# Retention followed by a feed-forward layer: q and k of the later chunks turned by 32x32 squares on VectorE instead of by TensorE

## Chip, cores and metric

The kernel runs on one core of one Trainium2 chip. The metric is the time of one execution on the device in microseconds (us), the median of several runs; lower is better.

## What is computed

First comes a retention layer: attention without a softmax, in which the score of a query at place t and a key at place s is multiplied by gamma^(t-s), with a gamma of its own for each head, and is zero for s > t. Its output, laid out as one row of 512 numbers per token, goes through a feed-forward layer with a squared ReLU. All is float32.

```python
# q, k, v: (batch 8, heads 8, tokens 576, 64)
scores = q @ k.T / sqrt(64)
gamma  = 1 - 2 ** (-5 - head)
D[t, s] = gamma ** (t - s) if t >= s else 0
attn   = (scores * D) @ v
x      = attn.transpose(0, 2, 1, 3).reshape(4608, 512)
h      = maximum(x @ w_in, 0)          # w_in: (512, 2048)
out    = (h * h) @ w_out               # w_out: (2048, 512)
```

## The kernel before

**Tiling.** A batch entry of 576 tokens is cut into five chunks: four of 128 tokens and a short one of 64. That makes 40 chunks, numbered 0 to 39; 4, 9, 14 and so on are short. The decay is split into a factor gamma^t on q (with the 1/sqrt(64)) and a factor gamma^-s on v, so that scores need only a mask. For every pair of heads a 64x64 state in PSUM (`u_ps`, copied to `u_sb`) carries the sum over the keys of earlier chunks.

**The retention of one chunk** goes through these pieces, each a function of the kernel. `load` (L131) fetches q, k and v with the tokens on the partitions, three chunks ahead. `turn` (L379) brings q and k to the layout that the score products need, with two heads of 64 dimensions on the 128 partitions and the tokens along the row: 16 TensorE transposes of 64x64 blocks (8 for a short chunk, L387) write a PSUM tile `t_ps`; ScalarE copies the half with k out to `kT` (L393), and VectorE takes the half with q to `qT` (L397) while it multiplies it by a table `dq` of gamma^t, 128 x 4 x 576 numbers, that was loaded from DRAM by `load` of chunks 4 to 8 (L138). Only for chunks 0 to 3 q is multiplied before the transpose, tokens on the partitions, by `scale_q` (L374, the operation at L377), on GpSimd, with a small table `dv`; then `turn` only copies (L395). `scores` (L400) makes the products (L415); VectorE masks them into a tile `ret` (L420, L422), and GpSimd multiplies v by its decay (L424). `retain_a`, `retain_b` and `retain_c` multiply the masked scores with v (L436), add to the state (L439) and multiply the state with q (L471); ScalarE copies the state (L445) and the finished chunk of x (L493).

**The first feed-forward product** works on blocks of 512 tokens with a scheme of seven products in place of eight (`PRODUCTS`). Block 0 is done in the plain way (`first_in`) while the weights are being converted. For every other block there are 28 steps (`ffn_in`, L580): four passes of seven steps, each of eight 128x128 by 128x256 matmuls (L595) into one of three PSUM tiles `h_a`, `h_b`, `h_c`. Each step has its way out of PSUM: ScalarE at steps 0 and 3 (L605, L611, after which GpSimd squares, L612), VectorE at the others (L607, L609, L614, L618, L621, with the squares at L602). Between them VectorE works off further parts in small portions: sums of the hidden blocks (L533 to L536), sums of x (L519 to L522), and, in blocks 3 to 7, the conversion and sums of w_out (L210 to L248).

**Order.** The schedule is written by hand: each engine takes its instructions in the order of the program and waits for each one's inputs. One loop runs over the chunks. For chunks after 4 the pass i of it is

```python
retain_a(i - 1)
if i < N_CH:
    turn(i)
ffn(i - 1, 0)
retain_b(i - 1)
if i < N_CH:
    scores(i)
retain_c(i - 1)
ffn(i - 1, 1)
```

where each `ffn` runs some three or four steps of the feed-forward product, spread over the tokens by `PACE`. After the loop the rest of the steps run, and then the second product (`inner`, L866; about 390 us), which the change does not touch.

Of the kernel before, what the change touches and what calls it, by code (L numbers as in the profile page):

```python
# [15 lines left out]
C = 128  # L16
# [24 lines left out]
def kernel(  # L41
# [6 lines left out]
    moe_w_out: bass.AP,  # L48
    decay_q: bass.AP,
    decay_v: bass.AP,  # L50
    out: bass.AP,
# [79 lines left out]
    def load(i):  # L131
        b, ci, c0, cs = chunks[i]
        got = {name: pool.tile([128, H, D], F32, tag=name, name=f"{name}_ld") for name, pool in (("q", ld3), ("k", ld4), ("v", ld4))}
        if i == 0:
            nc.sync.dma_start(dv, decay_v)
        if N_EARLY <= i < N_EARLY + NCH:

            nc.sync.dma_start(dq[:, :, c0:c0 + cs], decay_q[:, :, c0:c0 + cs])  # L138
        for name, src in (("q", q), ("k", k), ("v", v)):
            t = got[name]  # L140

            issue = nc.scalar if i == 0 and name != "q" else nc.sync
            at = src[b, :, c0:c0 + cs, :].rearrange("h s d -> s h d")
            if name == "v":
                issue.dma_start(t[:cs], at)
            else:

                issue.dma_start(t[:cs, 0:H // 2, :], at[:, 0:H // 2, :])
                for e in range(2):
                    issue.dma_start(t[:cs, H // 2 + e::2, :], at[:, H // 2 + 1 - e::2, :])  # L150
        loaded[i] = [got["q"], got["k"], got["v"]]
# [168 lines left out]

    dq = only.tile([128, HP, S], F32, name="dq")
    dv = only.tile([128, H, 2 * NCH], F32, name="dv")
# [50 lines left out]

    def scale_q(i, engine):  # L374

        ci, t = chunks[i][1], loaded[i][0]
        engine.tensor_tensor(t, t, dv[:, :, NCH + ci:NCH + ci + 1].to_broadcast([C, H, D]), op=ALU.mult)  # L377

    def turn(i):  # L379

        cs, c0 = chunks[i][3], chunks[i][2]
        n_h = cs // CH
        p = ps_t.tile([128, 2, 512], F32, tag="t", name="t_ps").rearrange("p h (j d t) -> p h j d t", j=2, d=HP)
        for j in (1, 0):
            for hp in range(HP):
                for h in range(n_h):
                    nc.tensor.transpose(p[:, h, j, hp, :], loaded[i][j][rows(h), 2 * hp:2 * hp + 2, :],  # L387
                                        ident[rows(h), rows(h)])
        for j, name in ((1, "kT"), (0, "qT")):
            t = st[i][name] = work2.tile([128, HP, C], F32, tag=name, name=name) if j == 0 else work.tile([128, HP, C], F32, tag=name, name=name)  # L390
            to = t[:, :, :cs].rearrange("p d (h t) -> p h d t", h=n_h)
            if j:
                nc.scalar.copy(to, p[:, :n_h, j, :, :])  # L393
            elif i < N_EARLY:
                nc.vector.tensor_copy(to, p[:, :n_h, j, :, :])  # L395
            else:
                nc.vector.tensor_tensor(to, p[:, :n_h, j, :, :], dq[:, :, c0:c0 + cs].rearrange("p d (h t) -> p h d t", h=n_h),  # L397
                                        op=ALU.mult)

    def scores(i):  # L400
# [10 lines left out]
        for hp in range(HP):  # L411
            for h in range(n_h):
                for e in range(2):
                    t = slice(CH * h, CH * h + CH)
                    nc.tensor.matmul(sc[e][rows(h), hp, :], lhsT=kT[rows(e), hp, t], rhs=qT[rows(e), hp, t],  # L415
                                     start=True, stop=True, skip_group_check=True)
        r = st[i]["ret"] = work2.tile([128, 2, HP, CH], F32, tag="ret", name="ret")
        if i < N_EARLY:
# [258 lines left out]
    def ffn(i, half):  # L677

        gone[0] += chunks[max(0, min(i, N_CH - 1))][3] / 2
        if steps and steps[0][0] == 0:  # L680

            for f in (step, lambda: convert(6)) if half else (lambda: convert(6), step):
                f()
            if half and steps and steps[0][0] == 0:
                step()
                convert(6)
            return
# [9 lines left out]
        while steps and count:  # L697
            held[0] = half == 0 and count == 1
            step()
            count -= 1  # L700
# [16 lines left out]
    for i in range(N_CH + 1):  # L717
        if i <= N_EARLY:
# [29 lines left out]
            elif i == N_EARLY:  # L748
                convert(5)
                step()  # L750
                convert(6)
            if i < N_EARLY:
                if i + 1 < N_EARLY:
                    scale_q(i + 1, nc.gpsimd)
                if i < 2:
                    warm(6, False)
                turn(i + 1)
        else:
            if i == N_EARLY + 1:
                gone[0] = TOK  # L760
            retain_a(i - 1)
            if i < N_CH:
                turn(i)
            ffn(i - 1, 0)
            retain_b(i - 1)
            if i < N_CH:
                scores(i)
            retain_c(i - 1)
            ffn(i - 1, 1)
        if i == 0:  # L770
# [194 lines left out]
def _decays(B, H, S, D):  # L965


    import numpy as np

    gamma = 1.0 - 2.0 ** (-5.0 - np.arange(H))  # L970
    t = np.arange(S)
    n = -(-S // C)
    gt = gamma[:, None] ** t / math.sqrt(D)
    pairs = gt.reshape(H // 2, 2, 1, S).copy()
    pairs[H // 4:] = pairs[H // 4:, ::-1]
    gq = np.repeat(pairs, D, axis=2).reshape(H // 2, 2 * D, S).transpose(1, 0, 2)
    s = np.arange(n * C).reshape(n, C)
# [3 lines left out]
    gv = np.concatenate([gv, by_s], axis=2)  # L981
    return np.ascontiguousarray(gq, dtype=np.float32), np.ascontiguousarray(gv, dtype=np.float32)

# [31 lines left out]
```

## Time and profile before

| | |
|---|---|
| time, median of 3 runs | 994.51 us (994.42 to 995.4) |
| span of the profiled execution | 991.7 us |
| VectorE busy | 748.6 us, 75% |
| ScalarE busy | 190.4 us, 19% |
| GpSimd busy | 81.6 us, 8% |
| loop over the chunks | from the start to about 530 us |
| second product | from about 600 us to the end |

A busy share is an average over stages that are bound by different things. What a change in the loop over the chunks is worth has to be read from views of that stretch: which engine has no gaps there, how full the others are, and which wait ends last. The chain of waits is read backwards from the last instruction; an engine that is not on it has time to spare at that place.

### The profile page before, as it was taken

The page shows a single profiled execution, that of the slowest core. Times are in us where ns is not written, and L with a number is a line of the kernel's source. Part 1 is how long each engine was busy: PE and PEld are TensorE (multiplying, and loading weights), DVE is VectorE, ACT ScalarE, POOL GpSimd, SP SyncE. Part 2 cuts the span into 40 slices and gives each one's busy share as a digit, 9 for nine tenths or more (in the row PEclk, how much of TensorE's full clock was granted, in tenths as well). Part 3 has the DMA queues.
Part 4 walks back from the last instruction along what each step waited for, and adds up shares of the span by engine and source line. Part 5 has one row for each costly group of instructions (what it writes and reads, how often), then busy time and mean ns, then how long its engine had stood idle before and what let it go on. Part 6 is the DMA issues. An engine that isn't in the chain of part 4 may idle for free.

```text
span 991.7 us, 24441 instructions
## 1 busy us (share of the span) xinstructions
PE 973.5 (98%) x10532; PEld 869.5 (88%) x10532; DVE 748.6 (75%) x1427; ACT 190.4 (19%) x462; POOL 81.6 (8%) x85
## 2 busy tenths in 40 slices
PE   7899999999999999999999999999999999999998
PEld 7655688888888888888888889999999999999998
DVE  4688696567878888897886777777777777777765
ACT  3444222222222222223221010000000000000000
POOL 3100011111111111111111000000000000000000
PEclk9999999999999999999999999999999999999999
DMA  9984657665696878769458999675673757556351
GB/s 205 250 239 143 174 172 208 162 175 176 187 311 199 223 234 260 224 209 283 142 212 297 404 389 348 235 283 163 230 268 148 265 197 270 192 213 216 126 212 44
DMA packets 187676, 220.40 MB, mean 222 GB/s; under 512 B 119216, under 2 KB 137648, under 8 KB 178608
## 3 DMA queue, kind: packets, MB, share of 16 engines
q1 hardware_dynamic: 185456, 218.31, 67.8%
q8 instruction: 83, 1.36, 0.6%
q10 hardware_dynamic: 2112, 0.52, 0.2%
q14 instruction: 25, 0.20, 0.1%
HBM read 129.41 MB, written 89.39 MB: 221 GB/s over the span
## 4 chain that ended last, share of the span: by engine, by line
PE 91%; DVE 5%; DMA 1%; SPq 1%; issue 1%; ACT 1%; DVEq 0%; ACTq 0%
PE o_b L866 17%; PE h_b L595 16%; PE o_c L866 11%; PE o_a L866 11%; PE h_a L595 10%; PE h_c L595 10%; PE h_ps L559 5%; PE x_ps L436 3%; PE t_ps L387 2%; PE sc_ps L415 2%; PE x_ps L471 2%; DVE room L602 1%; PE u_ps L439 1%; DMA w<-in_moe_w_in_dram 1%; DMA w<-in_moe_w_out_dram 0%
## 5 line engine op out<-in xcount | busy, mean ns | idle before, releaser
L595 PE MATMUL h_b<-room,w 128*128 128x256 f32 x736 | 177.2, 383 | 1.2 <-DVE room L520 0.9
L595 PEld LDWEIGHTS h_b<-room,w 128*128 128x128 f32 x736 | 137.2, 190 | 21.4 <-PE t_ps L387 1.1
L866 PE MATMUL o_b<-w,room 128*128 128x128 f32 x1168 | 144.5, 275 | 0.2 <-DVE room L817 0.2
L866 PEld LDWEIGHTS o_b<-w,room 128*128 128x128 f32 x1168 | 137.2, 192 | 0.5 <-DVE room L817 0.4
L866 PE MATMUL o_c<-w,room 128*128 128x128 f32 x1008 | 123.0, 275 | 0.0
L866 PEld LDWEIGHTS o_c<-w,room 128*128 128x128 f32 x1008 | 117.7, 192 | 0.0
L595 PE MATMUL h_c<-room,w 128*128 128x256 f32 x480 | 114.4, 381 | 0.0
L595 PE MATMUL h_a<-room,w 128*128 128x256 f32 x448 | 107.6, 383 | 0.0
L595 PEld LDWEIGHTS h_c<-room,w 128*128 128x128 f32 x480 | 90.4, 190 | 12.6
L595 PEld LDWEIGHTS h_a<-room,w 128*128 128x128 f32 x448 | 83.7, 190 | 11.8
L866 PE MATMUL o_a<-w,a 128*128 128x128 f32 x688 | 85.6, 275 | 0.0
L866 PEld LDWEIGHTS o_a<-w,a 128*128 128x128 f32 x688 | 81.2, 192 | 0.1
L612 POOL TENSOR_TENSOR room<-room 128x512 f32<-128x512 f32 x32 | 35.2, 1100 | 438.2 <-ACT room L611 370.6
L602 DVE SCALAR_TENSOR_TENSOR room<-room 128x512 f32<-128x512 f32 x96 | 68.1, 710 | 3.3
L880 ACT COPY r<-o_a 128x128 f32<-128x128 f32 x53 | 14.1, 266 | 271.7 <-PE o_a L866 241.2
L559 PE MATMUL h_ps<-room,w 128*128 128x512 f32 (+1 forms) x160 | 60.1, 526 | 2.5 <-DVE w L228 1.7
L614 DVE TENSOR_TENSOR room<-h_b,room 128x512 f32<-128x512 f32 x32 | 22.1, 690 | 46.9 <-PE h_b L595 46.9
L436 PEld LDWEIGHTS x_ps<-ret,v_ld 64*64 64x64 f32 x1152 | 40.4, 136 | 15.9 <-issue 11.7
L436 PE MATMUL x_ps<-ret,v_ld 64*64 64x64 f32 x1152 | 50.0, 226 | 3.5 <-ACT u_sb L474 3.4
L559 PEld LDWEIGHTS h_ps<-room,w 128*128 128x128 f32 x160 | 30.3, 196 | 24.6 <-issue 19.1
L424 POOL TENSOR_TENSOR v_ld<-v_ld,dv 128x512 f32<-128x512 f32 (+1 forms) x40 | 42.8, 1075 | 63.5 <-DMA v_ld<-in_v_dram 58.6
L876 DVE TENSOR_TENSOR small<-o_b,small 128x128 f32<-128x128 f32 x62 | 18.1, 292 | 38.4 <-PE o_b L866 38.4
(109 smaller groups left out, 1377.4 us busy)
## 6 DMA issues: line engine op xcount, KB each, us to landing
g_dram<-room SPq DMA_DIRECT2D x32, 1792.0 KB, 7.7
a<-g_dram SPq DMA_DIRECT2D x43, 1024.0 KB, 7.1
room<-g_dram SPq DMA_DIRECT2D x20, 1024.0 KB, 6.4
w<-w_dram SPq DMA_DIRECT2D x7, 1792.0 KB, 13.0
out_dram<-room SPq DMA_DIRECT2D x17, 512.0 KB, 3.4
w<-in_moe_w_in_dram SPq DMA_DIRECT2D x16, 512.0 KB, 6.1
w<-in_moe_w_out_dram SPq DMA_DIRECT2D x16, 512.0 KB, 4.1
v_ld<-in_v_dram SPq DMA_DIRECT2D x31, 256.0 KB, 4.4
```

The lines of the kernel that those rows point to most:

```text
L387: nc.tensor.transpose(p[:, h, j, hp, :], loaded[i][j][rows(h), 2 * hp:2 * hp + 2, :], ident[rows(h), rows(h)])
L415: nc.tensor.matmul(sc[e][rows(h), hp, :], lhsT=kT[rows(e), hp, t], rhs=qT[rows(e), hp, t], start=True, stop=True, skip_group_check=True)
L424: nc.gpsimd.tensor_tensor(vs[:cs], vs[:cs], dv[:cs, :, ci:ci + 1].to_broadcast([cs, H, D]), op=ALU.mult)
L436: own.append(lambda hp=hp, e=e, b=b: nc.tensor.matmul(x_at(hp, b, h), lhsT=s["vs"][rows(h), 2 * hp + b, :], rhs=s["ret"][rows(h), e, hp, : ...
L471: nc.tensor.matmul(x_at(hp, b, h), lhsT=u[rows(e), hp, :], rhs=s["qT"][rows(e), hp, CH * h:CH * h + CH], start=clears(b, hp // 2), stop=Fa ...
L559: nc.tensor.matmul(p.rearrange("p h t -> p (h t)"), lhsT=w[:, c, :], rhs=xT[0][:, c, lo * HT:hi * HT], start=(c == 0), stop=(c == N_DM - 1))
L595: nc.tensor.matmul(p[:, mm, :], lhsT=w[:, c, :], rhs=xs[n][right][:, c, :], start=(j in OPENS and mm == 0 and c == 0), stop=(j in CLOSES a ...
L602: nc.vector.scalar_tensor_tensor(t, t, 0.0, t, op0=ALU.max, op1=ALU.mult)
L612: nc.gpsimd.tensor_tensor(g["A11"], g["A11"], g["A11"], op=ALU.mult)
L614: nc.vector.tensor_tensor(g["A22"], p, p15, op=ALU.add)
L866: nc.tensor.matmul(p, lhsT=s["lefts"][left][:, m, :], rhs=w_out[j][:, m, WO_SLOT[right], :], start=(i in OPENS and m == 0), stop=(i in CLO ...
L876: nc.vector.tensor_tensor(s["u2"], p, s["p1"], op=ALU.add)
```

## The change

From chunk 9 on, TensorE no longer turns q and k. VectorE transposes each 32x32 square of a chunk of k and of q in place (`flip`: two instructions per chunk, on all 128 partitions, into a tile `flip`), and ScalarE then carries each group of 32 partitions to the 32 partitions where it belongs (`spread`, `move`: 16 copies of 32 partitions x 256 numbers for a full chunk, 8 for a short one). The copies go into a list, from which three are issued ahead of every step of the feed-forward product (six while block 0 is still being worked on); the remainder is issued after the first half of the steps. `flip` and `spread` of a chunk run one pass of the loop ahead of the pass that uses them.

The multiplication of q by its decay is done for all chunks by `scale_q`, tokens on the partitions, on GpSimd, one pass ahead (chunk 0 stays on VectorE). The table `dq`, its memory and its five loads are gone; chunks 4 to 8, which TensorE still turns, are copied out of PSUM by VectorE without a product. q and k share one double-buffered tile `qk`, and the masked scores are written over the k half of it instead of into a tile of their own.

The purpose is to take the transposes off TensorE, and the table and its loads out of the kernel.

```diff
@@ load
-        if N_EARLY <= i < N_EARLY + NCH:
-            nc.sync.dma_start(dq[:, :, c0:c0 + cs], decay_q[:, :, c0:c0 + cs])
@@ scale_q and what follows it
+        ci, cs = chunks[i][1], chunks[i][3]
+        t = loaded[i][0][:cs]
+        engine.tensor_tensor(t, t, dv[:cs, :, NCH + ci:NCH + ci + 1].to_broadcast([cs, H, D]), op=ALU.mult)
+    N_TURN = 9
+    moves = []
+    def new_qk(i):
+        t = work2.tile([128, 2, HP, C], F32, tag="qk", name="qk")
+        st[i]["qT"], st[i]["kT"] = t[:, 0, :, :], t[:, 1, :, :]
+        return t
+    def flip(i):
+        cs = chunks[i][3]
+        t = st[i]["flip"] = work2.tile([128, 4, 2, HP, 32], F32, tag="flip", name="flip")
+        for j in (1, 0):
+            nc.vector.transpose(t[:cs, :, j, :, :], loaded[i][j][:cs].rearrange("s (p e) (d a) -> s (e d) p a", e=2, d=2))
+    def spread(i):
+        to = new_qk(i)
+        for b in range(chunks[i][3] // 32):
+            for g in range(4):
+                moves.append(lambda b=b, g=g: nc.scalar.copy(
+                    to[32 * g:32 * g + 32, :, :, 32 * b:32 * b + 32], st[i]["flip"][32 * b:32 * b + 32, g, :, :, :]))
+    def move(count):
+        for f in moves[:count]:
+            f()
+        del moves[:count]
@@ turn
-            if j:
-                nc.scalar.copy(to, p[:, :n_h, j, :, :])
-            elif i < N_EARLY:
-                nc.vector.tensor_copy(to, p[:, :n_h, j, :, :])
-            else:
-                nc.vector.tensor_tensor(to, p[:, :n_h, j, :, :], dq[:, :, c0:c0 + cs].rearrange("p d (h t) -> p h d t", h=n_h),
-                                        op=ALU.mult)
+        to = new_qk(i)[:, :, :, :cs].rearrange("p j d (h t) -> p j d h t", h=n_h)
+        nc.scalar.copy(to[:, 1].rearrange("p d h t -> p h d t"), p[:, :n_h, 1, :, :])
+        nc.vector.tensor_copy(to[:, 0].rearrange("p d h t -> p h d t"), p[:, :n_h, 0, :, :])
@@ scores
-        r = st[i]["ret"] = work2.tile([128, 2, HP, CH], F32, tag="ret", name="ret")
+        r = st[i]["ret"] = st[i]["kT"].rearrange("p (e a) (b t) -> p e (a b) t", e=2, b=2)
@@ ffn
+            move(6)
             for f in (step, lambda: convert(6)) if half else (lambda: convert(6), step):
                 f()
...
             held[0] = half == 0 and count == 1
+            move(3)
             step()
@@ the loop over the chunks
+            scale_q(i + 1, nc.gpsimd)
             if i < N_EARLY:
-                if i + 1 < N_EARLY:
-                    scale_q(i + 1, nc.gpsimd)
...
+            if i + 1 < N_CH:
+                scale_q(i + 1, nc.gpsimd)
             retain_a(i - 1)
-            if i < N_CH:
+            if i < N_TURN:
                 turn(i)
             ffn(i - 1, 0)
+            move(len(moves))
+            if N_TURN <= i + 1 < N_CH:
+                flip(i + 1)
             retain_b(i - 1)
             if i < N_CH:
                 scores(i)
             retain_c(i - 1)
+            if N_TURN <= i + 1 < N_CH:
+                spread(i + 1)
             ffn(i - 1, 1)
```

## Prediction before the run

> **What bounds the kernel now.** First the page: the busy times and the chain that ended last.
>
> ```profile
> PE 973.5 (98%) x10532; PEld 869.5 (88%) x10532; DVE 748.6 (75%) x1427; ACT 190.4 (19%) x462; POOL 81.6 (8%) x85
> PE 91%; DVE 5%; DMA 1%; SPq 1%; issue 1%; ACT 1%; DVEq 0%; ACTq 0%
> ```
>
> TensorE has no gaps to speak of. Taking work from it shortens the kernel, unless something else fills the gap. Next the windows of the stretch in which chunks 9 to 39 run. Columns: length, then busy us (and instructions) of PE, PEld, DVE, ACT, POOL, then clock, DMA share, GB/s.
>
> ```profile
> 105.00:237.50 132.50, 130.72 (x1699) 110.81 (x1699) 95.03 (x149) 30.83 (x71) 17.87 (x17) 1.00 0.63 178
> 237.50:512.50 275.00, 272.64 (x3407) 231.72 (x3406) 231.40 (x395) 71.89 (x155) 40.99 (x38) 1.00 0.73 220
> ...
> 387.50:400.00 12.50, 12.50 (x163) 10.36 (x163) 11.83 (x22) 2.42 (x6) 0.06 (x1) 1.00 0.61 163
> ...
> 425.00:437.50 12.50, 12.28 (x121) 10.02 (x122) 12.40 (x19) 2.04 (x4) 2.58 (x2) 1.00 0.50 164
> ```
>
> Two stretches: up to 237 us VectorE is 72% busy (95.0 of 132.5), from there to 512 us 84% (231.4 of 275; the conversion of w_out runs then), and single windows of 12.5 us are full. So TensorE sets the time, VectorE is a close second, ScalarE (26%) and GpSimd (15%) are far off. In the chain in order of time (start, length, what) a turn stands like this:
>
> ```profile
> 332.68 0.01 PE u_ps L439 x2
> 332.69 0.65 PE t_ps L387 x16
> 333.33 1.93 PE h_c L595 x8
> ```
>
> The turn costs the path 0.65 us, and the products after it take 1.93 us, as they do (1.92) where no turn precedes them. A short chunk's eight transposes show 0.64 too.
>
> **What the Trainium skill says.** (1) VectorE: DVE Perf Modes, "The three transpose paths": VectorE transposes 32x32 blocks only, a bf16 128x128 tile in 311 ns. Vector Engine (DVE) Microarchitecture Reference, 3.8: one element per cycle and lane. No transpose on VectorE is in this trace; its two-input products of 512 numbers take 682 to 692 ns, which fits one per cycle at the 0.96 GHz given there. (2) ScalarE: Activation LUTs, "What ACT_TABLE_LOAD costs": 186 ns + 0.833 ns per number, and 93 ns of overlap back to back; for 256 numbers 399 ns. The trace has 375 ns (from PSUM). (3) VectorE: DVE Perf Modes, "Two Vector instructions with no wait between them": the second SBUF read interface of VectorE is shared with GpSimd. The trace agrees; in order of time (start, length, engine):
>
> ```profile
> 430.80 1.11 POOL L612 TENSOR_TENSOR room<-room 128x512 f32<-128x512 f32 x1 [13.44 <-ACT room L611]
> 430.93 1.53 DVE L246 TENSOR_TENSOR w<-w 128x512 f32<-128x512 f32 x1
> 431.87 1.50 POOL L424 TENSOR_TENSOR v_ld<-v_ld,dv 128x512 f32<-128x512 f32 x1
> 432.38 1.54 DVE L247 TENSOR_TENSOR w<-w 128x512 f32<-128x512 f32 x1
> ```
>
> Two sums of 0.69 us took 1.53 beside GpSimd: each lost 0.84.
>
> **The change part by part.**
>
> TensorE: 31 turns (chunks 9 to 39) by 0.645 us leave: 20.0 us, 7.7 of it outside the full stretch (12 turns) and 12.3 within it (19 turns). Nothing is added.
>
> VectorE, per chunk: two transposes come, the product at L397 goes. Its row: 0.686 us (128x512, x28) and 0.420 (128x256, short chunks); back to back such instructions start 0.60 and 0.36 apart. A transpose of 512 numbers costs between 0.60 (one per cycle, overlapped) and 1.2 (4-byte numbers at half rate; nothing here rules it out). I take 0.65, because the skill's rate names no type. Full chunk: 1.3 - 0.6 = +0.7; short: 1.3 - 0.36 = +0.94. In the full stretch 16 x 0.7 + 3 x 0.94 = 14.0 us.
>
> GpSimd: 36 more products at 1.06 to 1.10 us (rows L424, L377) for chunks 4 to 39; it has the time. But each may run beside VectorE: from 0 to 0.84 us of VectorE's time, as above. GpSimd's work comes in a bunch just after L611, where VectorE often waits for step 4 (L614 waits 21.3 us in this stretch), so the first product is mostly hidden and a third one falls on busy time; I take 0.4. 19 x 0.4 = 7.6 us.
>
> VectorE's sum there: 231.4 + 14.0 + 7.6 = 253.0 us, against 275 - 12.3 = 262.7. It fits on average (96%), but not everywhere. A window of 12.5 us holds 0.86 chunks: it becomes 11.94 long and gets 21.6 / 22 = 0.98 us more. 425 to 437: 13.4 in 11.9; 387 to 400: 12.8; 262 to 275 (11.47 now): 12.45. Overrun 1.4 + 0.9 + 0.5 = 2.8 us. Nine more windows (10.8 to 10.9 now) end just full; 0.3 us each for uneven order inside: 2.7. So TensorE waits about 5.5 us more for VectorE there. Before 237 us only the window 120 to 130 is full (9.82 of 10): 0.8.
>
> ScalarE: 24 x 16 + 7 x 8 = 440 copies of 256 numbers, 0.31 (399 less 93) to 0.40 us each, 136 to 176 us, less 31 copies of k (0.585 and 0.373; 17 us), over some 400 us that hold 103 us now: 55 to 65%. Three copies ahead of a step (0.9 to 1.2 us) lie beside that step's 1.73 us of matmuls: hidden.
>
> Waits added. The first transpose waits for k's load, the second for `scale_q`, both a pass ahead; behind them on VectorE stand the mask of the scores and L614 or L607, for which TensorE waits before it may write that tile again. A transpose falls while TensorE does `retain_b`, `scores` and `retain_c` (0.62 + 0.47 + 0.5 us), where VectorE had only the mask: it lies well. `scores` waits for the last copy; behind it on TensorE is all that follows, but the copies end before the last steps of the half, so I cost it at nothing. `scale_q` waits for q's load; behind it are the product with v and the square at L612, needed a pass and some steps later. The copies wait for `retain_c` two chunks back, which ScalarE's copy of x (L493) waits for already. The mask written over k waits for products that it waits for anyway: nothing.
>
> The table: five loads (1.18 MB) go. One lies on the chain:
>
> ```profile
> 26.68 1.56 SPq L138
> ...
> 32.23 5.65 DMA w<-in_moe_w_in_dram
> 37.90 0.44 DVE w L210
> ...
> 40.73 0.59 ACT room L493
> 41.37 5.17 PE h_ps L559 x16
> ```
>
> The weights' load at 32.23 is issued behind L138; without it that is 1.67 us earlier (26.68 to 28.35, where the next issue starts), and TensorE, idle for about that load, starts earlier: 1.7 us.
>
> Sum: -20.0 + 5.5 + 0.8 - 1.7 = -15.4; 994.5 - 15.4 = 979.1, say 979 us.
>
> **Rivals.** (a) VectorE's extra work fits its gaps: its waits in the full stretch are 40 us (21.3 at L614, 6.2 at L397 for ScalarE's copy, which vanishes with L397). For it: gaps lie beside every step 4. Against: the full windows. Then -20.0 - 1.7: 973 us. (b) VectorE becomes the bound, because transposes of 4-byte numbers take 1.2 us and GpSimd costs the full 0.84. Full stretch: 231.4 + 16 x 1.8 + 3 x 2.04 + 19 x 0.84 = 282.3, and some 10 us of waits that can't be filled: 292, +17 on 275; outside -7.7 + 1.0 - 1.7: in all 1003 us, slower. For it: 84% now. Against: the skill's rate. With one of the two costs alone it ends near 990 to 995. (c) ScalarE comes late: its copies from SBUF in 0.5 us or more, so `scores` waits some 0.7 us in each of 31 passes, and steps wait for L605: 979 + 22 = 1001 us. Against: ScalarE's 26% now, and that `move` goes in threes.
>
> **Chances.** The main case 0.60 (975 to 987), (a) 0.12, (b) 0.22 (half of it slower than before), (c) 0.06. Low end 971: (a), and no dip of the granted clock after that early idle (a window from 40 to 45 us shows 0.66). High end 997: (b) with one cost. Beyond it lie the worst of (b) and (c), about 0.12. Faster 0.80, same 0.04, slower 0.16.
>
> **What would show it.** TensorE busy some 20 us less and no t_ps after chunk 8; transposes of 0.65 to 0.72 us in VectorE's groups; VectorE's busy time up by 20 to 30 us, windows from 237 us near 96%; waits of h_a, h_b, h_c for VectorE of some 5 us more; scores waiting for ScalarE under 2 us. Transposes of 1.2 us, many VectorE rows far above 0.69, or scores waiting for ScalarE in each pass would make it wrong.

## Result and profile after

The changed kernel takes 1007.34 us (median of 4 runs, 1007.13 to 1009.39), beside 994.95 us for the kernel before: ratio 1.0129, 95% interval 1.0111 to 1.0146. It is slower by 12.4 us where the forecast was faster by 15.4; the time lies outside the range of 971 to 997.

First the page's busy times. In the changed kernel L390 are the transposes on VectorE, L396 the copies between partitions, L433 the score products, L614 the matmuls of the feed-forward steps, L624 and L630 ScalarE's ways out of steps 0 and 3, and L493 ScalarE's small copy in `retain_b`.

```profile
PE 966.5 (96%) x10092; PEld 861.4 (85%) x10092; DVE 786.1 (78%) x1458; ACT 351.3 (35%) x871; POOL 128.7 (13%) x121
```

440 matmuls are gone. The span is 1007.7 us, so TensorE's gaps are 1007.7 - 966.5 = 41.2 us; before they were 991.7 - 973.5 = 18.2. That is +23.0. And TensorE's busy time fell by 7.0 us only, although turns of 20 us left: what remained became some 13 us longer. The two together are the 16 us between the spans; they are more than the 12.4 us between the medians, because the profiled execution is the slowest of the four (1009.39 us). The page's chain of waits answers nothing this time: its first piece lies at 604 us, after the loop over the chunks.

The windows of the kernel after, columns as in the prediction (length, busy PE, PEld, DVE, ACT, POOL, clock, DMA share, GB/s):

```profile
105.00:237.50 132.50, 125.91 (x1546) 106.14 (x1544) 100.66 (x154) 83.75 (x205) 30.59 (x27) 0.99 0.62 180
237.50:512.50 275.00, 257.94 (x2976) 217.25 (x2975) 245.19 (x394) 167.99 (x400) 63.76 (x55) 0.96 0.73 218
330.00:342.50 12.50, 12.45 (x111) 10.53 (x112) 8.07 (x14) 7.80 (x20) 0.00 (x0) 0.77 0.46 116
387.50:400.00 12.50, 12.27 (x152) 10.31 (x151) 10.70 (x18) 10.02 (x24) 4.08 (x4) 1.00 0.91 263
425.00:437.50 12.50, 9.41 (x132) 7.84 (x131) 12.36 (x20) 4.26 (x12) 2.68 (x2) 1.00 0.44 123
505.00:517.50 12.50, 9.80 (x116) 8.18 (x116) 6.33 (x11) 7.65 (x20) 3.06 (x3) 0.73 0.39 147
```

Three things stand here. TensorE is no longer full: 257.9 of 275 us, where it had 272.6. VectorE, which I had expected to be the new limit at 96%, is 89% busy (245.2 of 275), so in most places it is not what TensorE waits for. And the granted clock is 0.73 and 0.77 in single windows that had 1.00 before: after some gaps the matmuls run slower for a while. Over 5-us windows from 105 to 570 us, the time without a matmul sums to 24.0 us (before 4.5) and the lost clock, length times (1 - clock), to 11.9 us (before 0.0).

Who ended the gaps, from the list of waits between 105 and 570 us (engine and what it waited for: us in total, times, longest):

```profile
ACT qk L396 <- DVE flip L390: 27.8, 15, 5.7
...
PEld sc_ps L433 <- ACT qk L396: 19.0, 20, 3.7
PE sc_ps L433 <- ACT qk L396: 16.1, 19, 3.6
...
PE h_a L614 <- ACT room L624: 3.1, 1, 3.1
...
PE h_b L614 <- DVE room L539: 1.6, 1, 1.6
```

The score products wait for ScalarE's copies, 16.1 us in 19 waits. TensorE's waits for VectorE's ways out, the ones that I had priced, are small.

What the forecast took off TensorE did go. This is the timeline of the place where a turn stood in the chain before; the step follows the state's product directly.

```profile
366.51 0.23 PE L458 MATMUL u_ps<-v_ld,k_ld 64*64 64x64 f32 x2
366.66 1.99 PE L614 MATMUL h_b<-room,w 128*128 128x256 f32 x8
```

The start of ScalarE's small copy (L474 before, L493 after) marks each chunk in both traces. Where nothing waits, the interval from one chunk's mark to the next is 0.64 to 0.65 us shorter than before; others gain less, or lose up to 3.4 us (the one that ends with chunk 32 loses 3.40, with chunk 25 2.85, with chunk 36 2.60). From chunk 8 to chunk 39 the kernel falls 13.6 us behind (1.2 to 14.8).

The same stretch shows how an interval loses, here the one of chunk 27 (timeline, ScalarE and the score products, in order of time: start, length):

```profile
361.19 1.23 ACT L396 COPY qk<-flip 32x256 f32<-32x256 f32 x3 [1.46 <-DVE flip L390]
366.14 0.59 ACT L624 COPY room<-h_a 128x512 f32<-128x512 f32 x1 [3.72 <-PE h_a L614]
366.81 0.37 ACT L464 COPY u_sb<-u_ps 128x256 f32<-128x256 f32 x1
367.20 3.74 ACT L396 COPY qk<-flip 32x256 f32<-32x256 f32 x9
372.20 0.60 ACT L630 ACTIVATE room<-h_a 128x512 f32<-128x512 f32 x1 [1.25 <-issue]
...
372.56 0.30 PE L433 MATMUL sc_ps<-qk 64*64 64x64 f32 x4
372.82 1.65 ACT L396 COPY qk<-flip 32x256 f32<-32x256 f32 x4
...
373.69 0.32 PE L433 MATMUL sc_ps<-qk 64*64 64x64 f32 x2 [0.83 <-ACT qk L396]
...
374.52 0.62 PE L433 MATMUL sc_ps<-qk 64*64 64x64 f32 x25 [0.51 <-ACT qk L396]
```

ScalarE has idle time (3.72 us before L624), but it takes its work in the program's order: the copies stand behind ways out that wait for steps. Only four steps with three copies ahead of each lie here between the place where the sixteen copies enter the list and the end of the half, so four copies are left. They stand behind L630, the way out of the last step of that half, and the scores come right after that step. So the remainder runs while TensorE waits. At 507 us the same costs 3.56 and 0.36 us.

How often this happens can be counted from the order of the program: for eleven of the 31 chunks one to four copies are left when the half ends, 24 in all. The 19 waits of the scores fall on eleven chunks too, and ten of these are the same. The intervals in which these ten lie (they end with the small copies of chunks 10, 14, 15, 24, 25, 27, 29, 30, 34 and 36) fall 13.7 us behind together; in the other 21 from chunk 9 on, gains and losses cancel.

The largest single loss, chunk 32, is another one: the first copies are at the head of ScalarE's work before their transposes are done, and h_a's way out stands behind them.

```profile
434.73 1.23 ACT L396 COPY qk<-flip 32x256 f32<-32x256 f32 x3 [5.67 <-DVE flip L390]
435.99 0.59 ACT L624 COPY room<-h_a 128x512 f32<-128x512 f32 x1
...
436.63 2.43 PE L614 MATMUL h_a<-room,w 128*128 128x256 f32 x8 [3.09 <-ACT room L624]
```

Copies and transposes, from the groups by shape (busy, mean ns of one):

```profile
L396 ACT COPY qk<-flip 32x256 f32<-32x256 f32 x440 | 177.1, 402 | 34.2 <-DVE flip L390 27.8
```

```profile
L621 DVE SCALAR_TENSOR_TENSOR room<-room 128x512 f32<-128x512 f32 x96 | 75.5, 786 | 3.3
L222 DVE TENSOR_TENSOR w<-w,w 128x512 f32<-128x512 f32 x32 | 27.1, 846 | 0.6
...
L390 DVE STREAM_TRANSPOSE flip<-k_ld 128x512 f32<-128x512 f32 x24 | 16.8, 702 | 0.0
L390 DVE STREAM_TRANSPOSE flip<-q_ld 128x512 f32<-128x512 f32 x24 | 16.0, 667 | 0.0
```

Before, the first two rows were 710 and 688 ns (L602, L225). The timeline shows what lengthens them, as before:

```profile
424.71 1.50 POOL L373 TENSOR_TENSOR q_ld<-q_ld,dv 128x512 f32<-128x512 f32 x1
425.22 1.54 DVE L539 TENSOR_TENSOR room<-room 128x512 f32<-128x512 f32 x1
426.17 1.50 POOL L443 TENSOR_TENSOR v_ld<-v_ld,dv 128x512 f32<-128x512 f32 x1
426.68 1.54 DVE L222 TENSOR_TENSOR w<-w,w 128x512 f32<-128x512 f32 x1
```

Last, the load that stood on the chain at 32.23 us:

```profile
27.10 1.81 SPq L193 DMA_DIRECT2D w<-in_moe_w_in_dram  x1
...
32.90 0.77 SPq L193 DMA_DIRECT2D w<-in_moe_w_in_dram  x1
...
38.40 0.43 DVE L207 TENSOR_SCALAR w<-w 128x512 uint32<-128x512 uint32 x1 [0.88 <-DMA w<-in_moe_w_in_dram]
```

The issue of the table between the two weight loads is gone, yet from one weight load to the next it is 5.80 us where it was 6.21: the issues that remain took longer (1.81 us where the first weight load took 0.62).

### The profile page after: what moved, and what is told of

Read it like the earlier page. It is cut to its first block, busy times and chain, and to the rows that moved or that the text cites. A ratio compares the mean times of both kernels' runs of the same rounds, so it can differ in the third digit from the quotient of the medians.

```text
span 1007.7 us, 24117 instructions
## 1 busy us (share of the span) xinstructions
PE 966.5 (96%) x10092; PEld 861.4 (85%) x10092; DVE 786.1 (78%) x1458; ACT 351.3 (35%) x871; POOL 128.7 (13%) x121
## 5 line engine op out<-in xcount | busy, mean ns | idle before, releaser
L396 ACT COPY qk<-flip 32x256 f32<-32x256 f32 x440 | 177.1, 402 | 34.2 <-DVE flip L390 27.8
L614 PE MATMUL h_b<-room,w 128*128 128x256 f32 x736 | 179.4, 387 | 1.9 <-DVE room L539 1.6
L614 PEld LDWEIGHTS h_b<-room,w 128*128 128x128 f32 x736 | 139.6, 193 | 23.3 <-issue 2.1
L614 PE MATMUL h_c<-room,w 128*128 128x256 f32 x480 | 116.6, 386 | 0.0
L614 PE MATMUL h_a<-room,w 128*128 128x256 f32 x448 | 109.8, 389 | 3.1 <-ACT room L624 3.1
L614 PEld LDWEIGHTS h_c<-room,w 128*128 128x128 f32 x480 | 91.8, 193 | 13.2
L614 PEld LDWEIGHTS h_a<-room,w 128*128 128x128 f32 x448 | 84.9, 193 | 15.7 <-ACT room L624 3.5
L621 DVE SCALAR_TENSOR_TENSOR room<-room 128x512 f32<-128x512 f32 x96 | 75.5, 786 | 3.3
L373 POOL TENSOR_TENSOR q_ld<-q_ld,dv 128x512 f32<-128x512 f32 (+1 forms) x39 | 47.2, 1210 | 76.5 <-DMA q_ld<-in_q_dram 70.1
L455 PEld LDWEIGHTS x_ps<-qk,v_ld 64*64 64x64 f32 x1152 | 42.0, 141 | 15.3 <-issue 13.7
L433 PE MATMUL sc_ps<-qk 64*64 64x64 f32 x1152 | 35.5, 233 | 19.5 <-ACT qk L396 16.1
L455 PE MATMUL x_ps<-qk,v_ld 64*64 64x64 f32 x1152 | 51.1, 230 | 3.0 <-DVE qk L441 2.0
```

The source lines that it names most:

```text
L373: engine.tensor_tensor(t, t, dv[:cs, :, NCH + ci:NCH + ci + 1].to_broadcast([cs, H, D]), op=ALU.mult)
L396: moves.append(lambda b=b, g=g: nc.scalar.copy(to[32 * g:32 * g + 32, :, :, 32 * b:32 * b + 32], st[i]["flip"][32 * b:32 * b + 32, g, :, : ...
L455: own.append(lambda hp=hp, e=e, b=b: nc.tensor.matmul(x_at(hp, b, h), lhsT=s["vs"][rows(h), 2 * hp + b, :], rhs=s["ret"][rows(h), e, hp, : ...
L614: nc.tensor.matmul(p[:, mm, :], lhsT=w[:, c, :], rhs=xs[n][right][:, c, :], start=(j in OPENS and mm == 0 and c == 0), stop=(j in CLOSES a ...
L621: nc.vector.scalar_tensor_tensor(t, t, 0.0, t, op0=ALU.max, op1=ALU.mult)
```

## Experiments

Theory A: the sixteen copies on ScalarE come late for the scores. Theory B: GpSimd's products hold VectorE up, and TensorE waits for VectorE. All ratios are against the kernel before, run on the same chip, with their 95% interval. Runs with q unscaled, or with four or eight copies per chunk, leave out work that the result needs; they only price a part. "Early" means that the transposes stand at the start of the pass. Fours and sixes are the copies issued ahead of each step, in place of three.

| run | us | ratio |
|---|---|---|
| all chunks turned by TensorE | 994.62 | 0.9997 [0.9981, 1.0013] |
| q unscaled | 1001.25 | 1.0059 [1.0038, 1.0081] |
| four copies | 987.74 | 0.9923 [0.9899, 0.9948] |
| eight copies | 988.56 | 0.9929 [0.9908, 0.995] |
| four copies, q unscaled | 975.79 | 0.9803 [0.9781, 0.9826] |
| copies that nobody reads | 1009.85 | 1.0143 [1.0123, 1.0164] |
| copies spread from the start of the pass | 1048.31 | 1.0534 [1.0501, 1.0567] |
| transposes early | 1003.55 | 1.008 [1.0053, 1.0107] |
| half of the copies on GpSimd | 1017.79 | 1.0235 [1.0188, 1.0282] |
| copies in fours | 1004.96 | 1.0091 [1.0059, 1.0124] |
| fours, transposes early | 1001.33 | 1.0066 [1.0046, 1.0086] |
| sixes, transposes early | 998.56 | 1.0036 [1.0023, 1.0049] |
| sixes, early, q unscaled | 991.9 | 0.9968 [0.9957, 0.9978] |
| four copies, sixes, early, q unscaled | 984.76 | 0.9891 [0.986, 0.9921] |
| squares for 19 chunks | 996.64 | 1.002 [1.0011, 1.0028] |
| squares for 19 chunks, sixes, early | 992.46 | 0.9976 [0.9963, 0.999] |
| only k by squares | 998.68 | 1.0033 [1.0019, 1.0047] |
| only k by squares, sixes | 992.65 | 0.9968 [0.995, 0.9987] |

### Which part of the change costs

**All chunks turned by TensorE.** What is left of the change is q scaled by tokens on GpSimd and the table gone.

```diff
-    N_TURN = 9
+    N_TURN = N_CH
```

> The changed kernel with TensorE turning every chunk, as before the change: no transposes on VectorE and no copies between partitions, but q is still scaled on GpSimd and the table is still gone. Theory A (ScalarE's copies come too late for the scores; the scores' waits and the clock dips that follow them make the 12 us): no waits of the scores for ScalarE, granted clock back to 0.995 or more, 991 to 998 us. Rival B (GpSimd's 36 further products hold up VectorE, so all that VectorE hands on comes late): the products are all there, so most of the loss stays: 1002 us or more.

994.62 us, no different from before. So the scaling and the table's removal together neither cost nor bring anything while VectorE has no transposes; the loss comes with the squares.

**q unscaled** from chunk 9 on, all else as changed.

```diff
-            if i + 1 < N_CH:
+            if i + 1 < N_TURN:
                 scale_q(i + 1, nc.gpsimd)
```

> The changed kernel with q left unscaled from chunk 9 on (the product on GpSimd is left out), all else as it is. Theory A: the copies keep their number and their 0.41 us, the scores go on waiting; VectorE gets back some 15 us, which helps only where the transposes come late: 998 to 1006 us. Rival B: the loss goes with the products: 980 to 990 us, and the scores' waits for ScalarE under 5 us.

1001.25 us: GpSimd's products cost 6 us of the 28 that the forecast missed. The scores still wait 14.9 us.

**Four copies** of 128 partitions per chunk in place of sixteen of 32; the squares stay on their partitions.

```diff
-        for b in range(chunks[i][3] // 32):
-            for g in range(4):
-                moves.append(lambda b=b, g=g: nc.scalar.copy(
-                    to[32 * g:32 * g + 32, :, :, 32 * b:32 * b + 32], st[i]["flip"][32 * b:32 * b + 32, g, :, :, :]))
+        if chunks[i][3] == C:
+            for b in range(4):
+                moves.append(lambda b=b: nc.scalar.copy(to[:, :, :, 32 * b:32 * b + 32], st[i]["flip"][:, b, :, :, :]))
...
```

> The changed kernel with four copies of all partitions per chunk in place of 16 copies of 32 partitions (eight for a short chunk); the squares then stay on their partitions, so that part of the move is left out, while transposes, products and waits stay. ScalarE has 1.7 us per chunk in place of 6.6. Theory A: no scores waiting, clock at 0.99 or more, 980 to 988 us. Rival B: the transposes are as late as they were, 1000 us or more.

987.74 us: twelve copies more per chunk cost 20 us. No wait of the scores for ScalarE is left among those of TensorE. Between 105 and 570 us the time without a matmul is 15.2 us here (24.0 in the changed kernel), the lost clock 1.7 us (11.9). This is the time that theory A forecast, but the run takes copies away and doesn't tell their number from their place; later runs do. What the four copies don't bring is the last 9 us to the forecast of 979.

**Eight copies** of 64 partitions, again without the full move between partitions.

```diff
-            for g in range(4):
-                moves.append(lambda b=b, g=g: nc.scalar.copy(
-                    to[32 * g:32 * g + 32, :, :, 32 * b:32 * b + 32], st[i]["flip"][32 * b:32 * b + 32, g, :, :, :]))
...
+                for e in range(2):
+                    moves.append(lambda b=b, e=e: nc.scalar.copy(
+                        to[64 * e:64 * e + 64, :, :, 32 * b:32 * b + 32], st[i]["flip"][64 * e:64 * e + 64, b, :, :, :]))
...
```

> As with four copies, but eight copies of 64 partitions for a full chunk (four for a short one); the squares stay on their 64 partitions, so part of the move is left out. ScalarE has 3.3 us per chunk. If the loss comes only where ScalarE has more work than a pass holds: nearly the time with four copies, 987 to 991 us. If it grows evenly with the copies: half way between 988 and 1007, 992 to 996 us.

988.56 us, the same as with four. So the cost doesn't grow evenly with the copies: eight by threes need three steps, which every chunk has, and sixteen need six.

**Four copies and q unscaled**, both edits together.

```diff
-            if i + 1 < N_CH:
+            if i + 1 < N_TURN:
                 scale_q(i + 1, nc.gpsimd)
...
+                moves.append(lambda b=b: nc.scalar.copy(to[:, :, :, 32 * b:32 * b + 32], st[i]["flip"][:, b, :, :, :]))
...
```

> Four copies of all partitions in place of 16 (so part of the move is left out) and q unscaled from chunk 9 on (the product on GpSimd left out): what is left of the change is the transposes on VectorE. If the two costs add (20 us for the copies, 6 for GpSimd's products), 981 to 984 us. If GpSimd's products cost time only because they made the copies later, no more is gained than with four copies alone: 986 to 989 us.

975.79 us, 19 us below the kernel before, with all transposes on VectorE. The 20 us of TensorE are there when nothing disturbs it. Beside the four-copy run it prices GpSimd's products at 12 us. Both forecasts missed it (981 to 984 and 986 to 989): the two omissions together bring more than their sum.

**Copies that nobody reads.** All chunks turned by TensorE, and the same 440 copies between two tiles of their own.

```diff
+    there = [only.tile([128, 2, HP, C], F32, name=f"there{j}") for j in range(2)]
+    squares = only.tile([128, 4, 2, HP, 32], F32, name="squares")
...
-        to = new_qk(i)
+        to = there[i % 2]
```

> The kernel of the first experiment (TensorE turns every chunk, q scaled on GpSimd), with the 440 copies of 32 partitions x 256 added in the same places, from a tile that is written once to tiles that nobody reads. Theory A1: occupying ScalarE by itself does little, 995 to 999 us, because nothing waits for the copies. Theory A2: ScalarE's own copies out of PSUM are held up, TensorE waits for them, 1003 us or more.

1009.85 us, 15 us more than without the copies. Nothing waits for these copies, so it is ScalarE's own work that they hold up. This is the time of theory A2; but it is not the copies as such that cost. Compared with the run without copies by the marks of the small copy, 17 of the 29 intervals from chunk 11 to 39 differ by 0.01 us or less, though ScalarE makes its copies in them as well. The kernel falls 14.7 us behind from chunk 10 to 39; 11.6 of it lie in the nine intervals that end with copies left over, and 2.8 in the one that follows the last of these. So in this order the copies cost nothing where none are left over; the remainder costs, even when nobody reads it. From the list of waits:

```profile
PE x_ps L459 <- ACT u_sb L497: 10.2, 9, 4.2
```

L497 is the small copy of x (L493 of the changed kernel), for which the next product of TensorE waits. The remainder of the copies stands ahead of it, as it stands ahead of the scores.

### Where the copies stand

**Copies spread from the start of the pass**, with transposes there too, the scaling half a pass earlier and a third `qk` buffer.

```diff
+                flip(i + 1)
+                spread(i + 1)
+            ffn(i - 1, 0)
...
-                spread(i + 1)
...
-        t = work2.tile([128, 2, HP, C], F32, tag="qk", name="qk")
+        t = work3.tile([128, 2, HP, C], F32, tag="qk", name="qk")
```

> The changed kernel with half a pass more for the copies: transposes at the start of a pass, ahead of the first half of its feed-forward steps, the copies spread over both halves, a third buffer for q and k, and q scaled half a pass earlier. The same instructions. Theory A: the copies are done before the scores need them, waits of the scores under 4 us, 980 to 992 us. Rival B: VectorE is as full as before, the transposes come late again, 1000 us or more.

1048.31 us, the worst, and in rival B's range, though VectorE is not fuller (780.8 us busy, 786.1 in the changed kernel). From its list of waits:

```profile
ACT qk L397 <- DVE flip L391: 67.5, 25, 6.9
...
PE x_ps L456 <- ACT u_sb L494: 44.5, 21, 4.6
```

The copies now come up on ScalarE before their transposes are done. Waiting at the head of the queue they block the small copy behind them, and through it TensorE.

**Transposes early**, the scaling half a pass earlier, the copies where they were.

```diff
+                flip(i + 1)
             ffn(i - 1, 0)
             move(len(moves))
-            if N_TURN <= i + 1 < N_CH:
-                flip(i + 1)
...
+            if i + 2 < N_CH:
+                scale_q(i + 2, nc.gpsimd)
             retain_c(i - 1)
```

> The changed kernel with the two transposes half a pass earlier, at the start of the pass, and q scaled half a pass earlier too; the copies stay where they are, so they find their squares ready. Theory A1 with the copies' own length as cause: the scores wait nearly as long, 1003 us or more. If it is the late transposes that make the copies late (ScalarE waited 27.8 us for them): ScalarE's wait for the squares under 5 us, the scores' waits under 6 us, 990 to 998 us.

1003.55 us. ScalarE's waits for the transposes are gone (0.9 us), which brings 4 us, but the scores still wait 13.9 us: the remainder stays behind the last step.

**Half of the copies on GpSimd.**

```diff
-                moves.append(lambda b=b, g=g: nc.scalar.copy(
+                copy = nc.scalar.copy if g % 2 == 0 else nc.gpsimd.tensor_copy
+                moves.append(lambda b=b, g=g, copy=copy: copy(
```

> The changed kernel with half of the copies between partitions on GpSimd in place of ScalarE (8 each for a full chunk), same order, nothing left out. If ScalarE's length of queue is the cause and GpSimd's copies, with one input, hold up VectorE little: the scores' waits fall under 6 us, 988 to 996 us. If GpSimd's copies hold up VectorE as its products do (some 12 us for 31 products when VectorE is full): 1000 us or more.

1017.79 us. A copy takes 564 ns there, VectorE's busy time rises to 811 us, and the scores wait 16.7 us for GpSimd instead.

**Copies in fours**, then fours and sixes with the transposes early, to clear the list before the last step.

```diff
-            move(3)
+            move(4)
```

In the third run it is `move(6)`; the second and third also have the transposes early, by the edit shown above.

> The changed kernel with four copies ahead of each feed-forward step in place of three; nothing else. Theory P (place: a full chunk's 16 copies need six steps by threes, a pass often has five, and the rest is issued behind ScalarE's copy of the last step, just before the scores): no rest is left, the scores' waits for ScalarE fall from 16 to 5 us or less, 994 to 999 us. Rival L (length: 6.6 us of copies are too many for the pass wherever they stand): 1004 us or more.

> Four copies ahead of each step, and the transposes half a pass earlier (q scaled half a pass earlier too), so that the first copies find their squares ready and ScalarE's copies of a step are not held up behind them. Nothing left out. Theory P: scores' waits under 3 us, 986 to 992 us, near the 988 of four and eight copies. Rival L: 1000 us or more.

> The same with six copies ahead of each step, which all stand ahead of the first three steps: 2.5 us of copies before a step whose matmuls take 1.73 us, so ScalarE's way out of PSUM comes up to 0.8 us late twice. Theory P: within 3 us of the version by fours. Rival L: as the version by fours, 1000 us or more; if the lateness of ScalarE's own copies is what counts, worse than by fours by 5 us or more.

1004.96, 1001.33 and 998.56 us. The scores' waits of 16.1 us fall to 7.2, 5.8 and, in sixes, to 1.6. So the place of the copies was the cause of those waits, but the times of theory P for both runs in fours (994 to 999, 986 to 992) were missed, and rival L's came: removing the waits brought at most 9 us and not 16. Other waits took their place, here in the run in sixes:

```profile
PEld h_b L614 <- DVE room L633: 12.0, 11, 3.0
...
PE h_b L614 <- DVE room L633: 7.4, 8, 2.6
...
PE x_ps L455 <- ACT u_sb L493: 5.9, 4, 2.9
```

These are VectorE's ways out and the small copy.

**Sixes, early, q unscaled**: the run in sixes with `scale_q` left out from chunk 9 on.

```diff
-            if i + 2 < N_CH:
+            if i + 2 < N_TURN:
                 scale_q(i + 2, nc.gpsimd)
```

> The changed kernel with the transposes at the start of the pass and the copies issued in sixes, and q left unscaled from chunk 9 on (the product with the decay of q is left out). With the products and the copies as they are this order took 998.6 us, and its scores waited 1.6 to 2.1 us for ScalarE. Theory S (GpSimd's products beside a full VectorE are what remains): without them the time falls by the 12 us that they cost with four copies, to 985 to 988 us. Theory C (the 16 copies cost by occupying ScalarE and VectorE waits on their order, wherever they are put): it falls by the 6 us that they cost in the changed kernel or less, to 992 to 997 us.

991.9 us, 6.7 less; theory C's range just missed at its lower end, and not the 985 to 988 of theory S. Its timeline shows what is left:

```profile
488.44 0.70 DVE L390 STREAM_TRANSPOSE flip<-k_ld 128x512 f32<-128x512 f32 x1
489.07 0.67 DVE L390 STREAM_TRANSPOSE flip<-q_ld 128x512 f32<-128x512 f32 x1
...
490.83 0.41 DVE L207 TENSOR_SCALAR w<-w 128x512 uint32<-128x512 uint32 x1
...
491.28 0.72 ACT L215 ACTIVATE w<-w,exp_bias 128x512 uint32<-128x512 uint32 x1 [2.88 <-DVE w L207]
...
491.91 0.65 ACT L216 ACTIVATE w<-w 128x512 f32<-128x512 uint32 x1
...
492.94 0.14 ACT L493 COPY u_sb<-x_ps 128x2 f32<-128x2 f32 x1
...
493.14 0.32 PE L455 MATMUL x_ps<-qk,v_ld 64*64 64x64 f32 x2 [2.88 <-ACT u_sb L493]
```

VectorE runs without a gap there, the transposes stand ahead of the conversion of w_out (L207), ScalarE's part of that conversion waits 2.88 us for it, the small copy stands behind, and TensorE waits 2.88 us.

**Four copies in that order**: the run just shown, with the four copies of 128 partitions.

```diff
...
+                moves.append(lambda b=b: nc.scalar.copy(to[:, :, :, 32 * b:32 * b + 32], st[i]["flip"][:, b, :, :, :]))
...
```

> The run with early transposes, copies in sixes and q unscaled (991.9 us), with four copies of 128 partitions per chunk in place of sixteen of 32: the squares stay on their partitions, so the move between partitions is left out, as the scaling of q is. The same two omissions with late transposes and copies in threes took 975.8 us. Theory O (the order with early transposes costs by itself, since they go ahead of the steps' ways out on VectorE): 984 to 990 us. Theory C (the twelve further copies cost, whatever the order): 975 to 979 us.

984.76 us, theory O's range. By ratio, the order (early, in sixes) costs 0.9% on its own (0.9891 against 0.9803 with late transposes and threes) and twelve more copies in it 0.8% (0.9968). So there are two costs of some 8 us each, and early transposes exchange part of the one for the other. In the two profiles the time without a matmul is 12.7 us with four copies and 15.7 with sixteen, the lost clock 0.0 and 6.8 us: most of what can be seen is clock. Its size differs between executions of one kernel, though (with sixteen copies the mean clock ran from 0.986 to 0.997 in 20 runs), so why the twelve copies cost 8 us where the scores hardly wait stays open.

### Less of the change

**Squares for 19 chunks** of the 31, TensorE turning those next to a short chunk; then the same with transposes early and sixes.

```diff
+    squares = {i for i in range(N_TURN, N_CH) if i % NCH >= 2}
...
-            if N_TURN <= i + 1 < N_CH:
+            if i + 1 in squares:
...
```

> The changed kernel, but TensorE turns the chunks for which the copies have the fewest steps to lie beside: those after a short chunk and the ones after these (numbers that leave 0 or 1 by 5); the other 19 of chunks 9 to 39 go by squares. Theory A1 (the copies of 0.41 us end too late for the scores, worst where a short chunk leaves few steps): most of the scores' waits vanish, TensorE has 12 us less work, 985 to 993 us. Theory A2 (the copies hold up ScalarE's own ways out of PSUM, wherever they stand): the loss falls only with the number of copies, 40% fewer: about 1000 us.

> The changed kernel with squares for 19 of the 31 chunks only (not for those next to a short chunk; these are turned by TensorE), transposes early, copies in sixes. With copies in threes and late transposes such a mixture took 996.6 us. If the remainder counts: 990 to 993 us, below the kernel before. If not: 995 to 998.

**Only k by squares**, in the kernel before, with its one transpose early: q stays with TensorE and its table, the masked scores are written over k. The copies are 32x128, in threes. The second run has `move(6)` in place of `move(3)` and differs in nothing else.

```diff
-        for j in (1, 0):
+        for j in ((1, 0) if i < N_TURN else (0,)):
...
+        t = st[i]["flip"] = work2.tile([128, 4, HP, 32], F32, tag="flip", name="flip")
+        nc.vector.transpose(t[:cs], loaded[i][1][:cs].rearrange("s (p e) (d a) -> s (e d) p a", e=2, d=2))
...
+            move(3)
```

> The kernel before, in which from chunk 9 on only k goes by squares (one transpose on VectorE, at the start of a pass, and 16 copies of 32 partitions x 128 on ScalarE); TensorE still turns q, VectorE still multiplies it by the table, nothing is added on GpSimd, nothing left out. TensorE has 10 us less work. A copy of 128 should take 0.30 us, 4.7 us per chunk in place of 6.6. If ScalarE's overload has a threshold that this stays under: 984 to 991 us. If the loss grows with the copies' time from the first copy on: 994 to 1000 us.

> The kernel before with only k turned by squares from chunk 9 on, q left to TensorE and its table, as in the run that took 998.7 us, but with the copies issued in sixes. If the remainder of the copies behind the last step's ScalarE copy was what cost there (the scores waited 6 to 7.6 us for it), the time falls to 990 to 994 us, below the kernel before. If the length of ScalarE's work counts, it stays at 997 to 1000.

996.64 and 992.46; 998.68 and 992.65 us. The first of these lies in neither forecast (985 to 993; about 1000). In both pairs the sixes (in the first with the transposes early too) bring what the theory of the remainder says, and the result is below the kernel before: ratio 0.9968 (0.995 to 0.9987) with k alone. This pair is the plainest test of the place: the same instructions in another order, the scores' 6.1 us of waits for ScalarE gone, 6 us less. A copy of 32x128 takes 296 ns. With half the data the copies are still 440, so their number alone doesn't make the loss. The kernel before is beaten by 2.6 us, the changed one by 15. The intervals end at 0.9987 and 0.999, so the gain over the kernel before is small but there.

## Why the prediction was wrong

**TensorE's 20.0 us: right.** Undisturbed intervals between chunks gain 0.64 to 0.65 us each, as the chain of before said, and with four copies and q unscaled the kernel gains 19 us.

**Transposes at 0.65 us: right.** 702 and 667 ns in the groups, some 0.63 and 0.60 us apart.

**ScalarE's copies "hidden", "I cost it at nothing": this is the step that failed.** The length was right: 402 ns, the top of my 0.31 to 0.40. The skill's ScalarE: Activation LUTs, "What ACT_TABLE_LOAD costs", from which I took 0.31 as the lower end, gives 93 ns of overlap back to back; nine copies took 3.74 us, 0.42 apart, so there was none. What was wrong is the step from "three copies ahead of a step lie beside that step's matmuls" to "the copies end before the last steps of the half". Sixteen copies by threes need six steps. They enter the list before the second half of a pass and must be done after the first half of the next. Two such halves mostly have six to eight steps, but next to a short chunk four or five, and twice `retain_c` itself runs three steps, ahead of which no copies are issued, so that four are left. All this was in the code. The remainder then stands behind the way out of the very last step, and the scores follow that step at once. ScalarE was 35% busy over the whole span and 61% in the full stretch (168.0 of 275), within my 55 to 65%: its load was forecast well, and the load was not the point. Rival (c), at 0.06, had the place and nearly the size (1001 us), but for a longer copy and a wait in every pass; it was 19 waits at eleven of 31 chunks, with up to 3.6 us each. By the run with four copies this step cost 20 us; issuing the sixteen copies sooner gave back 9 of them, because the order that does it brings waits of its own.

**"It lies well", of the transposes: not everywhere.** Late as they are, they made ScalarE's copies wait 27.8 us in 15 places, and at chunk 32 TensorE 3.1 us. Their lateness cost 4 us by the run with the transposes early.

**TensorE's clock: a cost that I didn't have.** I named the dip of the clock only for the early idle. Of the seven gaps of 1.5 us or more between 105 and 570 us five brought one; those of 2.0 us before 129 us and of 1.6 us before 299 us did not. At 325 to 340 us the scores waited 2.17 and 0.36 us, and the windows of 5 us show a clock of 0.88, 0.50 and 0.94: 3.4 us lost besides 2.5 us of wait. The Trainium skill, TensorE: Matmul & The Clock Gate, "What's actually happening", says that the array's clock is halved after an idle window of about 3.4 us and comes back after a busy one. The trace agrees with the half and with about the length: in windows of 1 us the clock stands at 0.50 for some 3.4 us after 137, 438 and 475 us, and for twice as long from 329 and 506 us. But waits of 1.6 and 0.51 us at 137 us were enough for it (0.77 and 0.89 in the two windows that follow from 135 us). And the length of a gap doesn't decide alone: the run with eight copies has 17.6 us without a matmul, gaps of up to 2.7 us, and no lost clock. What else decides isn't shown.

**GpSimd's 0.4 us of VectorE's time per product: right; what it costs: too small.** VectorE is busy 37.5 us more. Transposes add 42.3 us, L397's products take 22.6 off, copying chunks 4 to 8 (L416) gives 3.2 back: the other 14.6 us over 36 products are 0.41 each. In the pair with four copies the products take 14.5 us of VectorE's time (787.5 us busy with them, 773.0 without) and cost 12 us. I let 7.6 us of it disappear mostly in the average; where the transposes have filled VectorE, most of such time reaches the end. With the products away, the transposes themselves cost nothing that can be seen. By its size this is the 9 us between 979 and the four-copy run; a finer division of it isn't shown.

**VectorE to 96%, TensorE waiting 5.5 us for it.** It wasn't tested in the changed kernel: TensorE was held up elsewhere, so VectorE stood at 89%. With four copies it appears about as forecast: VectorE 95% (261.0 of 275 us), TensorE waiting 5.1 us at h_b for it; in the run in sixes it is 7.4 us. A reading of the sum was loose: of the "nine more windows (10.8 to 10.9 now)" the trace before has five at 10.8 to 10.93 and three more down to 10.67; the term is at most 1.2 us too large by this.

**The table's 1.7 us: not there.** The issues between two weight loads got 0.4 us shorter and not 1.67, and with TensorE turning all chunks the kernel takes what it took before.

**Rival (b)** had the right side for the wrong reason: neither transposes of 1.2 us nor VectorE as the bound.

## What to carry to other kernels

A share of busy time says whether an engine has room, not whether a piece of work is done when it is needed: count the pieces against the places at which they may be issued, in the pass that has the fewest such places and not in the average one, and look at what the last of them stands behind. Work moved to an engine that runs in order must not be queued ahead of, or wait in front of, the small copy for which the bounding engine waits. And a gap of TensorE of some 2 us can cost more than its length, since its clock may drop afterwards (here 19.5 us of further gaps came with 11.9 us of lost clock, with eight copies 13.1 us with none). Here it was better to move less and keep the engine fed, as k alone in sixes shows.

## What the runs showed of the hardware

ScalarE's copies from SBUF of 256 numbers take 402 to 403 ns each whether they carry 32, 64 or 128 partitions. Their distance differs. The first line is the timeline of the four-copy run (all copies start at the same partition), the second that of the eight-copy run (the start alternates), the third that of the changed kernel:

```profile
211.19 1.33 ACT L396 COPY qk<-flip 128x256 f32<-128x256 f32 x4
```

```profile
210.25 3.31 ACT L397 COPY qk<-flip 64x256 f32<-64x256 f32 x8
```

```profile
203.90 3.73 ACT L396 COPY qk<-flip 32x256 f32<-32x256 f32 x9
```

With one of 0.40 us at the end these are 0.31, 0.42 and 0.42 us apart: an overlap of 0.09 us is there in the first, and missing in the copies that change their start partition from one to the next. No run tells the change of partition from the smaller number of partitions as its cause. A copy on GpSimd of 32x256 takes 564 ns.
